# Linear attention and SwiGLU on one core: token tile 2 loaded one weight chunk earlier, its Newton steps on GpSimd, its normalisation behind one more phi(K), a phi(K) and a V cast ahead of its transpose copy

## The chip, the cores and the metric

One core of a Trainium2 chip. The metric is the device time of one execution in microseconds. Each execution is recorded with a state, fast or slow, by its time and the clock granted to TensorE. The profile's span runs from the first to the last instruction; in every profiled run here the device time is about 1.8 us more than the span.

In the profile, PE is TensorE (PEld its weight loads), DVE VectorE, ACT ScalarE, POOL GpSimd and SP SyncE; a q behind a name marks the queue that issues its instructions. PSUM is the memory that the matmuls write to, in banks, and SBUF the one that holds the other tiles on the chip.

## The reference

A linear attention block (32 heads of 32) over a layer-normalised input of 2048 tokens and 1024 features, gated by a SwiGLU block of width 3584:

```python
xn = _layernorm(x)
q, k, v = split_heads(xn @ wqkv)
phi = lambda t: jnp.where(t > 0, t + 1, jnp.exp(t)) + 1e-6
kv = einsum("bhsd,bhse->bhde", phi(k), v);  z = einsum("bhsd->bhd", phi(k))
o  = (phi(q) @ kv) / (phi(q) @ z + 1e-6)
s  = o @ wo
g  = silu((silu(xn @ w_gate) * (xn @ w_up)) @ w_down)
return x + s * g
```

(Shortened here; shapes and the random inputs are left out.)

## The kernel before

Tokens come in 16 tiles of 128, the K/V weights (1024 x 2048) in four chunks of 512 columns: 0 and 1 give K, 2 and 3 give V. For each tile: statistics, 1/sqrt by three Newton steps of four operations each (tiles 0 and 1: by a square root on ScalarE), normalisation, transposition; then for each chunk eight matmuls into a PSUM bank, and an evacuation (phi for K, a cast for V). Below, "product (i, c)" is tile i times chunk c.

The loads, in the order of the sync queue (half of x tile 0 and the whole of x tile 1 go on ScalarE's queue):

```python
load_x(0)
load_x(1)
load_wkv(0, halves=2 if DC % 2 == 0 else 1)
nx = 2
for c in range(1, NCH):
    load_wkv(c)
    if nx < NT and c != 2:
        load_x(nx)
        nx += 1
for i in range(nx, NT):
    load_x(i)
```

Newton, three times, on the engine that is named (GpSimd if none is):

```python
def emit_rstd(gid, eng=None):
    eng = eng or nc.gpsimd
    ...                             # cut: three preparations on nc.vector
    for _ in range(NR_ITERS):       # 3
        eng.tensor_tensor(out=w, in0=y, in1=y, op=ALU.mult)
        eng.tensor_tensor(out=w, in0=w, in1=a, op=ALU.mult)
        eng.tensor_scalar(out=w, in0=w, scalar1=-0.5, scalar2=1.5, op0=ALU.mult, op1=ALU.add)
        eng.tensor_tensor(out=y, in0=y, in1=w, op=ALU.mult)
```

(Slices cut.) Evacuation of K: ScalarE makes `e_t` = exp and `r_t` = relu out of PSUM, which frees the bank; VectorE adds eps to `r_t` and makes `pk_sb` of both, which frees `e_t` and `r_t`. There are two buffers each of `e_t` and `r_t`, and three PSUM banks for products (branches for other tiles are cut):

```python
nc.scalar.activation(out=e_t[:], in_=t_ps, func=ACT.Exp)
nc.scalar.activation(out=r, in_=t_ps, func=ACT.Relu)
nc.vector.tensor_scalar(out=r, in0=r, scalar1=EPS, scalar2=None, op0=ALU.add)
nc.vector.scalar_tensor_tensor(out=dst, in0=e_t[:], scalar=1.0, in1=r, op0=ALU.min, op1=ALU.add)
```

Every engine works through its instructions in the order in which they are emitted. That order at the start of the kernel (what comes before and after is cut):

```python
emit_Bmm(0, 0)          # eight matmuls of tile 0, chunk 0
emit_TR(1)              # transposes on PE, copies out of PSUM
ln_pre(2, nc.vector)    # statistics and Newton of tile 2
emit_Bev(0, 0)          # evacuation
emit_Bmm(1, 0)
emit_N(2)               # normalisation on VectorE
emit_Bmm(0, 1)
emit_Bev(1, 0)
emit_Bev(0, 1)
emit_Bmm(1, 1)
emit_Bmm(0, 2)
emit_TR(2)              # copy out of PSUM on ScalarE
emit_Bev(1, 1)
emit_Bev(0, 2)
emit_Bmm(1, 2)
emit_Bev(1, 2)
ln_pre(3)
emit_Bmm(2, 0)
```

Of the kernel before, what the change touches and what calls it, by code (L numbers as in the profile page):

```python
# [21 lines left out]
def kernel(  # L22
# [11 lines left out]
    nc = tc.nc  # L34
# [7 lines left out]
    NT = S // P  # L42
# [75 lines left out]
    def xn_ap(dcs, tok):  # L118
        b = tok.start // TB
        return xn_blk_tiles[b][:, dcs, tok.start - b * TB:tok.stop - b * TB]  # L120
# [24 lines left out]
    def emit_phi(work, t_ps, dst, W, in_place=False, act=False):  # L145
        e_t = work.tile([P, W], FP32, name="e_t", tag="e_t")
        if act:
            nc.scalar.activation(out=e_t[:], in_=t_ps, func=ACT.Relu, scale=-1.0)
            nc.scalar.activation(out=e_t[:], in_=e_t[:], func=ACT.Exp, scale=-1.0)
            nc.scalar.activation(out=t_ps, in_=t_ps, func=ACT.Relu)  # L150
            phi_late.append(lambda: nc.vector.scalar_tensor_tensor(out=dst, in0=e_t[:], scalar=EPS, in1=t_ps,
                                                                   op0=ALU.add, op1=ALU.add))
            return
        nc.scalar.activation(out=e_t[:], in_=t_ps, func=ACT.Exp)
        if in_place:
            r = t_ps
            nc.vector.tensor_scalar(out=r, in0=t_ps, scalar1=0.0, scalar2=EPS, op0=ALU.max, op1=ALU.add)
        else:
            r_t = work.tile([P, W], FP32, name="r_t", tag="r_t")
            r = r_t[:]  # L160
            nc.scalar.activation(out=r, in_=t_ps, func=ACT.Relu)
            nc.vector.tensor_scalar(out=r, in0=r, scalar1=EPS, scalar2=None, op0=ALU.add)
        nc.vector.scalar_tensor_tensor(out=dst, in0=e_t[:], scalar=1.0, in1=r,
                                       op0=ALU.min, op1=ALU.add)
# [198 lines left out]
    with ExitStack() as p1:  # L363
# [15 lines left out]
        def x_ap(i):  # L379
            return xp_tiles[i // 4][:, i % 4, :]  # L380
# [3 lines left out]
        def load_x(i):  # L384
            if i == 0 and D % 2 == 0:
                h = D // 2
                x_loads[i] = nc.sync.dma_start(out=x_ap(i)[:, 0:h], in_=x2[0:P, 0:h])
                nc.scalar.dma_start(out=x_ap(i)[:, h:D], in_=x2[0:P, h:D])
                return
            if i == 1:  # L390
                x_loads[i] = nc.scalar.dma_start(out=x_ap(i), in_=x2[i * P:(i + 1) * P, :])
                return
            x_loads[i] = nc.sync.dma_start(out=x_ap(i), in_=x2[i * P:(i + 1) * P, :])

        def load_wkv(c, halves=1):
            hs = DC // halves
            return [nc.sync.dma_start(out=wkv_sb[:, h * hs:(h + 1) * hs, c * CW:(c + 1) * CW],
                                      in_=wqkv_v[:, h * hs:(h + 1) * hs, D + c * CW: D + (c + 1) * CW])
                    for h in range(halves)]
# [3 lines left out]
        load_x(0)  # L403
        load_x(1)
        load_wkv(0, halves=2 if DC % 2 == 0 else 1)
        nx = 2
        for c in range(1, NCH):
            load_wkv(c)
            if nx < NT and c != 2:
                load_x(nx)  # L410
                nx += 1
        for i in range(nx, NT):
            load_x(i)
        def load_qo(wt, wv, c):
# [18 lines left out]
        def grp_of(i):  # L433
            return grp_tiles(i)[0]

        def grp_tiles(gid):
            return (gid,) if gid < 6 else (gid - gid % 2, gid - gid % 2 + 1)

        def emit_stats(i):
            gid = grp_of(i)  # L440
            if gid not in grp_state:
                mv = small.tile([P, TPB, AGG], FP32, name="mv", tag="mv")
                rstd = small.tile([P, TPB], FP32, name="rstd", tag="rstd")
                grp_state[gid] = (mv, rstd, grp_tiles(gid))
            mv, rstd, tiles = grp_state[gid]
            k = tiles.index(i)
            stats = small.tile([P, NSC, nc.vector.BN_STATS_DIM], FP32, name="stats", tag="stats")
            xr = x_ap(i).rearrange("p (c f) -> p c f", f=SCH)
            sts = [nc.vector.bn_stats(out=stats[:, c, :], in_=xr[:, c, :]) for c in range(NSC)]
            nc.vector.bn_aggr(out=mv[:, k, :], in_=stats[:])  # L450
            ln_state[i] = (mv, rstd, k)
            return sts
# [31 lines left out]
        def emit_norm(i, dst, cols=None):  # L484
            mv, rstd, k = ln_state[i]
            src = x_ap(i) if cols is None else x_ap(i)[:, cols]
            return nc.vector.tensor_scalar(out=dst, in0=src, scalar1=mv[:, k, 0:1], scalar2=rstd[:, k:k + 1],
                                           op0=ALU.subtract, op1=ALU.mult)
# [3 lines left out]
        def emit_N(i):  # L492
            xn = xnw.tile([P, D], BF16, name="xn", tag="xn")
            xn_tiles[i] = xn
            if i < 2:
                for hh in range(2):
                    cols = slice(hh * (D // 2), (hh + 1) * (D // 2))
                    emit_norm(i, xn[:, cols], cols=cols)
            else:
                emit_norm(i, xn[:])  # L500
            ln_state.pop(i)
            if i >= NPE:
                xn_tiles.pop(i)
                nc.sync.dma_start_transpose(out=xn_ap(slice(0, DC), slice(i * P, (i + 1) * P)), in_=xn[:])

        def emit_TR(i):
            tok = slice(i * P, (i + 1) * P)
            xn = xn_tiles.pop(i)
            nh = 2 if i < 2 else 1
            dch = DC // nh  # L510
            for hh in range(nh):
                tr_ps = psC.tile([P, dch, P], BF16, name="tr_ps", tag="C")
                for dc in range(dch):
                    nc.tensor.transpose(tr_ps[:, dc, :], xn[:, (hh * dch + dc) * P:(hh * dch + dc + 1) * P], ident[:])
                dst = xn_ap(slice(hh * dch, (hh + 1) * dch), tok)
                if i == 1 and hh == 0:
                    nc.vector.tensor_copy(out=dst, in_=tr_ps[:])
                else:
                    nc.scalar.copy(out=dst, in_=tr_ps[:])  # L519
# [5 lines left out]
        def emit_Bmm(i, c):  # L525
            tok = slice(i * P, (i + 1) * P)
            kv_ps = psB.tile([P, CW], FP32, name="kv_ps", tag="B")
            kv_banks[(i, c)] = kv_ps
            for dc in range(DC):
                mm = nc.tensor.matmul(kv_ps[:], lhsT=xn_ap(dc, tok), rhs=wkv_sb[:, dc, c * CW:(c + 1) * CW],  # L530
                                      start=(dc == 0), stop=(dc == DC - 1))
                if dc == 0 and c == 0:
                    marks[("B", i)] = mm

        def emit_Bev(i, c):
            kv_ps = kv_banks.pop((i, c))
            if i not in pkv_tiles:
                pk_sb = work.tile([P, D], BF16, name="pk_sb", tag="pk_sb")
                pkv_tiles[i] = (pk_sb, v_bufs[i % 2])
            pk_sb, v_sb = pkv_tiles[i]  # L540
            if c < NCC:
                emit_phi(phiw, kv_ps[:], pk_sb[:, c * CW:(c + 1) * CW], CW, in_place=i >= 9)
            else:
                vc = c - NCC
                nc.scalar.copy(out=v_sb[:, vc * GPC:(vc + 1) * GPC, 0:P],
                               in_=kv_ps[:].rearrange("p (g c) -> p g c", c=P))
# [10 lines left out]
        def ln_pre(i, eng=None):  # L557
            emit_stats(i)
            if i == grp_tiles(i)[-1]:
                emit_rstd(grp_of(i), eng)  # L560
# [13 lines left out]
        emit_N(1)  # L574
        emit_Bmm(0, 0)
        emit_TR(1)
        ln_pre(2, nc.vector)
        emit_Bev(0, 0)
        emit_Bmm(1, 0)
        emit_N(2)  # L580
        emit_Bmm(0, 1)
        emit_Bev(1, 0)
        emit_Bev(0, 1)
        emit_Bmm(1, 1)
        emit_Bmm(0, 2)
        emit_TR(2)
        emit_Bev(1, 1)
        emit_Bev(0, 2)
        emit_Bmm(1, 2)
        emit_Bev(1, 2)  # L590
        ln_pre(3)
# [845 lines left out]
```

## Time and profile before

| what | value |
|---|---|
| device time, median of the three runs ahead of the prediction | 758.95 us (758.80 to 758.96) |
| the execution that the profile was taken of | 759.85 us, span 758.1 us |
| PE busy | 750.5 us, 99% |
| PE busy before 27 us | 23.75 of 27 us |

The lines that carry the argument stand in the prediction. In a line of a timeline, the first two numbers are start and length in us, then come engine, source line, operation, output<-input, shape and count, and in brackets the idle time of the engine in front of it and what ended it.

### The profile page before, as it was taken

Reading aid. Unit: us, or ns where it says so; the run is one execution under the profiler, and the core shown is the slowest. Engines: PE = TensorE matmul, PEld = TensorE weight load, DVE = VectorE, ACT = ScalarE, POOL = GpSimd, SP = SyncE. Lnnn points to the kernel's source line nnn. Section 1 sums busy time; section 2 is a strip of 40 time slices with the busy share of each in tenths; the row PEclk is TensorE's granted clock in tenths of the full one; section 3 lists DMA queues with packets and bytes.
Section 4 is the critical chain, followed back from the end, with each engine's and each line's share of the span. In section 5 each row is a group of like instructions: output and inputs, shape, how many; then the busy total and the mean of one; then the engine's idle time right before and its main releaser. Section 6 shows DMA issues by size and latency. Waiting matters only on the chain.

```text
span 758.1 us, 10498 instructions
## 1 busy us (share of the span) xinstructions
PE 750.5 (99%) x3731; PEld 348.8 (46%) x3731; DVE 559.8 (74%) x1043; ACT 376.0 (50%) x526; POOL 274.9 (36%) x340
## 2 busy tenths in 40 slices
PE   8999999999999999999999999999999999999997
PEld 3444444454454444444444444444444444444443
DVE  6787787887687778888889775368676777787335
ACT  4678767889966666656658311132323223211122
POOL 0435799998540266868585000100000000200000
PEclk9999999999999999999999999999999999999999
DMA  9767799869688668878799236398644445430824
GB/s 315 256 179 153 198 337 306 311 148 280 198 195 284 229 225 295 296 280 316 265 330 398 106 108 247 125 371 326 230 176 167 167 166 175 178 134 15 278 87 135
DMA packets 105845, 170.30 MB, mean 225 GB/s; under 512 B 34816, under 2 KB 82176, under 8 KB 95168
## 3 DMA queue, kind: packets, MB, share of 16 engines
q1 hardware_dynamic: 100144, 144.99, 59.3%
q0 software_dynamic: 4208, 22.15, 7.5%
q10 hardware_dynamic: 1440, 2.49, 1.0%
q8 instruction: 29, 0.48, 0.3%
q14 instruction: 24, 0.20, 0.1%
HBM read 111.67 MB, written 50.59 MB: 214 GB/s over the span
## 4 chain that ended last, share of the span: by engine, by line
PE 95%; DVE 2%; DMA 1%; ACT 1%; issue 0%; SPq 0%; ACTq 0%; DVEq 0%
PE zw L941 26%; PE kv_ps L530 13%; PE xb L941 13%; PE dzw L1126 12%; PE yb L941 6%; PE q_ps L183 6%; PE dx L1126 6%; PE dy L1126 3%; PE fx L792 3%; PE s_ps L750 3%; DMA xp<-in_A_x_dram 1%; PE kvz L552 1%; PE nd L719 1%; PE df L1126 1%; DVE w_sb L283 0%; PE fx L750 0%
## 5 line engine op out<-in xcount | busy, mean ns | idle before, releaser
L941 PEld LDWEIGHTS <-w_sb 128*128 128x128 f16 (+1 forms) x1568 | 152.2, 98 | 182.7
L941 PE MATMUL xb<-xnT,w_sb 128*128 128x512 bf16 x448 | 115.0, 379 | 0.0
L530 PE MATMUL kv_ps<-wkv_sb,xnT 128*128 128x512 bf16 x512 | 114.0, 379 | 1.0 <-ACT xnT L519 0.5
L941 PE MATMUL zw<-xnT,w_sb 128*128 128x512 bf16 x448 | 105.8, 379 | 0.0
L941 PE MATMUL zw<-S,w_sb 128*128 128x512 f16 x448 | 105.8, 379 | 0.0
L295 POOL TENSOR_TENSOR w_sb<-w_sb 128x512 f16<-128x512 bf16 x42 | 50.2, 1195 | 95.7 <-DVE w_sb L283 51.3
L260 ACT ACTIVATE w_sb<-w_sb 128x2048 bf16<-128x2048 bf16 x42 | 79.9, 1902 | 3.8 <-DMA w_sb<-in_B_w_up_dram 2.8
L1126 PE MATMUL dx<-w_sb,hT 128*128 128x512 bf16 x210 | 79.6, 379 | 0.0
L530 PEld LDWEIGHTS <-xnT 128*128 128x128 bf16 x512 | 48.3, 97 | 56.7 <-ACT xnT L519 0.9
L1126 PEld LDWEIGHTS <-hT 128*128 128x128 bf16 (+1 forms) x462 | 44.7, 98 | 52.3
L183 PE MATMUL q_ps<-xnT,wq_sb 128*128 128x512 bf16 x256 | 58.4, 379 | 0.0
L1126 PE MATMUL dzw<-w_sb,hT 128*128 128x512 f16 x196 | 58.3, 379 | 0.0
L1017 ACT ACTIVATE sg<-cg 128x1024 bf16<-128x1024 f32 x28 | 29.6, 1057 | 57.2 <-DVE cg L1010 57.2
L941 PE MATMUL yb<-S,w_sb 128*128 128x512 f16 x224 | 57.4, 378 | 0.0
L1010 DVE SCALAR_TENSOR_TENSOR cg<-zw,rc_all,s 128x1024 f32<-128x1024 f32 x28 | 35.9, 1284 | 25.9 <-PE zw L941 14.0
L969 DVE SCALAR_TENSOR_TENSOR s<-yb,rc_all,s 128x512 f32<-128x512 f32 x42 | 31.5, 749 | 27.5 <-ACT s L968 27.5
L296 POOL TENSOR_TENSOR w_sb<-w_sb 128x512 f16<-128x512 bf16 x42 | 50.5, 1202 | 3.3
L1066 POOL TENSOR_TENSOR hs<-hT 128x512 f16<-128x512 bf16 x2 | 2.5, 1247 | 132.6 <-ACT sg L1017 132.6
L298 POOL TENSOR_TENSOR w_sb<-w_sb 128x512 f16<-128x512 bf16 x42 | 50.3, 1197 | 0.0
L297 POOL TENSOR_TENSOR w_sb<-w_sb 128x512 f16<-128x512 bf16 x42 | 50.2, 1196 | 0.0
L1100 POOL DMA_DIRECT2D out_dram<-io x16 | 8.7, 542 | 101.9 <-DVE io L1099 101.6
L968 ACT ACTIVATE s<-xb,rcl 128x512 f32<-128x512 f32 x14 | 9.6, 688 | 65.0 <-PE xb L941 65.0
(183 smaller groups left out, 1186.1 us busy)
## 6 DMA issues: line engine op xcount, KB each, us to landing
w_sb<-pk_g SPq DMA_DIRECT2D x27, 1024.0 KB, 5.9
pk_g<-w_sb SPq DMA_DIRECT2D x14, 1024.0 KB, 5.0
w_sb<-wd SPq DMA_DIRECT2D x14, 1024.0 KB, 5.6
w_sb<-pk_u SPq DMA_DIRECT2D x14, 1024.0 KB, 5.0
pk_u<-w_sb POOLq DMA_DIRECT2D x13, 1024.0 KB, 5.4
w_sb<-wd SPq DMA_DIRECT2D x14, 768.0 KB, 5.6
w_sb<-in_B_w_gate_dram SPq DMA_DIRECT2D x14, 512.0 KB, 6.4
w_sb<-in_B_w_down_dram SPq DMA_DIRECT2D x28, 256.0 KB, 4.9
```

The costliest lines, as they stand in the source:

```text
L183: nc.tensor.matmul(q_ps[:], lhsT=wq_sb[:, dc, g * P:(g + 1) * P], rhs=xn_ap(dc, btok), start=(dc == 0), stop=(dc == DC - 1))
L260: nc.scalar.activation(out=junk, in_=raw_view(key, t), func=ACT.Square, accum_out=asum[:])
L295: nc.gpsimd.tensor_tensor(out=T1, in0=b12, in1=b11, op=ALU.subtract)
L296: nc.gpsimd.tensor_tensor(out=T2, in0=b22, in1=T1, op=ALU.subtract)
L297: nc.gpsimd.tensor_tensor(out=T3, in0=b22, in1=b12, op=ALU.subtract)
L298: nc.gpsimd.tensor_tensor(out=T4, in0=b21, in1=T2, op=ALU.subtract)
L530: mm = nc.tensor.matmul(kv_ps[:], lhsT=xn_ap(dc, tok), rhs=wkv_sb[:, dc, c * CW:(c + 1) * CW], start=(dc == 0), stop=(dc == DC - 1))
L941: mm = nc.tensor.matmul(out, lhsT=lhs(k), rhs=rhs(k), start=(first and k == 0), stop=(k == HK - 1), skip_group_check=True)
L969: nc.vector.scalar_tensor_tensor(out=s2[:], in0=y_[:], scalar=rc, in1=s1[:], op0=ALU.mult, op1=ALU.add)
L1010: nc.vector.scalar_tensor_tensor(out=d12, in0=zw[:], scalar=rc, in1=s2[:, None, :].to_broadcast([P, 2, TB]), op0=ALU.mult, op1=ALU.add)
L1017: nc.scalar.activation(out=sg[:, 1:3, :], in_=cf[:], func=ACT.Silu)
L1126: nc.tensor.matmul(out, lhsT=lhs, rhs=rhs, start=first, stop=lastk, skip_group_check=True)
```

## The change

Its intent: let tile 2 arrive earlier, free VectorE of twelve small operations that stand in front of the first phi(K), and let ScalarE free PSUM banks before it copies tile 2's transpose.

```diff
         load_wkv(0, halves=2 if DC % 2 == 0 else 1)
-        nx = 2
+        load_x(2)
+        nx = 3
         for c in range(1, NCH):
             load_wkv(c)
-            if nx < NT and c != 2:
-                load_x(nx)
-                nx += 1
@@
         emit_TR(1)
-        ln_pre(2, nc.vector)
+        ln_pre(2)
         emit_Bev(0, 0)
         emit_Bmm(1, 0)
-        emit_N(2)
         emit_Bmm(0, 1)
         emit_Bev(1, 0)
+        emit_N(2)
         emit_Bev(0, 1)
         emit_Bmm(1, 1)
         emit_Bmm(0, 2)
-        emit_TR(2)
         emit_Bev(1, 1)
         emit_Bev(0, 2)
+        emit_TR(2)
         emit_Bmm(1, 2)
```

The matmuls and transposes of PE keep their order.

## The prediction

> **What bounds the kernel now.** I read the page first (engine shares, then the chain by engine), then busy time by stretch, then the chain in order of time over the start, and last the timelines of PE, DVE and GpSimd (POOL) around the edited code.
>
> From the page, parts 1 and 4:
>
> ```profile
> PE 750.5 (99%) x3731; PEld 348.8 (46%) x3731; DVE 559.8 (74%) x1043; ACT 376.0 (50%) x526; POOL 274.9 (36%) x340
> PE 95%; DVE 2%; DMA 1%; ACT 1%; issue 0%; SPq 0%; ACTq 0%; DVEq 0%
> ```
>
> The reader is to see that PE bounds the kernel: 95% of the chain that ended last. So a change of this kind, which removes no matmul, can only win idle time of PE. Busy time by stretch says where that is:
>
> ```profile
> 0.00:27.00 27.00, 23.75 (x123) 10.86 (x124) 16.62 (x58) 12.31 (x21) 2.90 (x20) 1.00 1.00 333
> 27.00:150.00 123.00, 123.00 (x694) 60.11 (x692) 100.32 (x218) 94.23 (x154) 91.39 (x140) 1.00 0.83 241
> ```
>
> (The columns after the length are busy time of PE, PEld, DVE, ACT, POOL; then clock, DMA share and GB/s.) From 27 to 150 us PE is never idle; before 27 us it lacks 3.25 us. The edit touches only this first stretch. What it wins there, the dense stretch behind it hands on unchanged, since everything later is tied to matmuls and not to the clock on the wall.
>
> The chain in order of time, start us and length us:
>
> ```profile
> 2.75 9.32 DMA xp<-in_A_x_dram
> ...
> 12.10 1.30 DVE stats L449 x2
> ...
> 16.52 0.35 DVE r_t L162
> 16.89 0.70 DVE pk_sb L163
> ...
> 17.69 0.60 ACT e_t L154
> ...
> 20.26 0.50 ACT r_t L161
> ...
> 20.80 5.34 PE kv_ps L530 x24
> ```
>
> The chain is not on PE before 20.80. It is: token tile 2 lands at 12.08; its statistics and Newton steps hold DVE, in order, until 16.5; only then DVE makes the first phi(K) (pk_sb), which frees the buffer that ACT's next exponential waits for, and ACT in turn frees the PSUM banks. PE's timeline shows what that costs:
>
> ```profile
> 10.20 7.08 PE L530 MATMUL kv_ps<-wkv_sb,xnT 128*128 128x512 bf16 x32 [0.30 <-DVE xnT L517]
> 18.09 0.62 PE L514 MATMUL tr_ps<-ident,xn 128*128 128x128 bf16 x8 [0.81 <-DVE xn L487]
> 18.83 7.31 PE L530 MATMUL kv_ps<-wkv_sb,xnT 128*128 128x512 bf16 x32
> ```
>
> A matmul takes 0.38 us but follows its forerunner after (7.08-0.38)/31 = 0.216 us; a transpose after (0.62-0.22)/7 = 0.057. So 32 matmuls from 10.20 let PE go on at 17.11; the transposes of tile 2 start at 18.09 (0.98 lost, waiting for the normalised tile). They would let PE go on at 18.55; it starts at 18.83 (0.28 lost, bank still read by ACT). Eight matmuls later, at 20.56, tile 2's first product could start, and the chain has it at 20.80 (0.24 lost, bank again). **Lost: 1.50 us.** That is the most that these parts of the change can win.
>
> **What the Trainium skill says.** "Perfetto Trace Analysis", section "Identifying the Most-Contended Engine": matmul busy share is a poor measure of headroom because matmuls are pipelined. The trace agrees: PE's busy row charges only 0.81 us to the transposes' wait, the starts show 0.98, and the two bank waits are in no row. Hence I reckon in start times.
>
> "DMA: Bandwidth & Descriptors", section "Queues, rings and completion order": on each DMA engine descriptors are consumed in ring order. So an earlier issue on the same queue means an earlier landing, paid by whatever it overtook. The trace agrees: tile 2, issued right behind chunk 1 of the K/V weights, landed 0.7 us after it (below).
>
> "SBUF — State Buffer", section "Who interferes with whom": a DVE instruction with two SBUF inputs, or in a 2-port mode, and a GpSimd one that reads SBUF exclude each other for a whole instruction. The trace agrees; DVE and POOL timelines:
>
> ```profile
> 30.25 0.69 DVE L163 SCALAR_TENSOR_TENSOR pk_sb<-e_t,r_t 128x512 bf16<-128x512 f32 x1
> 30.26 0.72 POOL L479 TENSOR_TENSOR lnw<-lnw,lna 128x1 f32<-128x1 f32 x1
> ```
>
> Usually the same POOL step takes 0.19. So Newton steps on POOL beside phi(K) on DVE will be stretched.
>
> **The change part by part.**
>
> Part 1, the load order. Two weight chunks, each alone in its stretch of the DMA view (size, us to landing): chunk 1, issued at 2.21, and chunk 2, issued at 4.31.
>
> ```profile
> wkv_sb<-in_A_wqkv_dram SPq DMA_DIRECT2D x1, 1024.0 KB, 9.2
> wkv_sb<-in_A_wqkv_dram SPq DMA_DIRECT2D x1, 1024.0 KB, 10.8
> ```
>
> Chunk 1 lands at 11.4, tile 2 at 12.08 (2.75+9.32), chunk 2 at 15.1. The second half of chunk 0 (issued 1.66, 6.7 to landing) is there at 8.4. Swapped, tile 2 lands at about 8.4+0.7 = 9.1 and chunk 1 at 12.08; bytes in front of chunk 2 are the same, so all later loads stay. Chunk 1 is first needed by the ninth of the 32 matmuls, at 10.20+8x0.216 = 11.93. Now it starts at about 12.12: **0.19 us of new wait**.
>
> Part 2, statistics. DVE's last work before them is the copy of tile 1's transpose, which ends at 10.14. They start at 10.16 instead of 12.10, 1.94 us earlier.
>
> Part 3, Newton. On DVE the twelve steps run from 14.23 to 16.52, so leaving takes 2.3 us out of DVE's queue. On POOL, tile 3's undisturbed run gives the price:
>
> ```profile
> 24.03 0.19 POOL L478 TENSOR_TENSOR lnw<-rstd 128x1 f32<-128x1 f32 x1 [22.65 <-DVE rstd L474]
> ...
> 27.03 0.19 POOL L482 TENSOR_TENSOR rstd<-rstd,lnw 128x1 f32<-128x1 f32 x1
> ```
>
> That is 0.273 us a step against 0.193 on DVE. The last DVE preparation starts at 14.04-1.94 = 12.10, the first POOL step 0.24 later (as 23.79 to 24.03) at 12.34, the last 3.00 later, and the normalisation 0.22 after that (27.03 to 27.25): 15.56 undisturbed. But DVE now does four phi(K) operations in that time: ACT's relus end at 12.92 and 13.91, so DVE works from 12.95 to about 15.2. Tile 4's POOL run, beside the same four operations, took 4.16 us between first and last step (29.88 to 34.04) instead of 3.00. That gives 16.72; laying the steps against the four operations one by one gives 16.87. I take 16.8. The normalisation lasts 0.54, so tile 2 is ready at 17.35.
>
> Part 4, the order of emission. Normalising tile 2 behind tile 1's first phi(K) keeps DVE from idling in front of phi(K) while POOL works. Moving tile 2's transpose copy on ACT behind the phi of (tile 1, chunk 1) and the V cast of (tile 0, chunk 2) gives PSUM banks back first. PE's own order is unchanged. Check of the path: the first phi(K) is done at 14.1 (before: 17.6), ACT's next exponential starts there and its bank is free at 15.3; the next pair ends at about 16.9; the V cast at about 18.1 (0.41 behind the last matmul, as 24.04 to 24.45, plus 0.6); the transpose copy takes 1.01 more, to about 19.1.
>
> Sum for PE: matmuls 9 to 32 run from 12.12 to 17.30. Transposes start at 17.40, 0.05 after the tile is ready (0.10 lost). The next eight matmuls start at 17.86 (bank free since 15.3). Tile 2's first product starts at 19.59; its copy ended at 19.1, its bank at 16.9. Before it was 20.80: **1.2 us won** of the 1.50, with 0.19 lost to the weights and 0.10 to POOL. 758.95-1.2 = 757.75; I say **757.7 us**.
>
> Behind that I looked for something that does not move. Chunk 3 lands at 18.1 and is needed at 21.3; tile 3 is in by 19; its normalisation gets earlier. Tile 4 comes by DMA transpose: it landed at 38.0, needed at 40.0, and its input also gets earlier. Nothing there takes the gain back.
>
> **The rivals.** (a) Weights take the place of the tile: chunk 1 comes later than 12.12, say 12.6 to 13, because the longer issue stalls on the sync queue (tile 2's issue took 1.5 us, chunk 3's 3.9) hit it. For: PE has only 0.5 us of slack there now. Against: issue is far ahead of landing. It would leave 0.5 to 0.9 us: 758.0 to 758.4. (b) POOL becomes the bound: the steps end at 17.5 or later, through the lock or a slow start after long idling. For: the 0.72 us steps. Against: tile 3's first step, after 22.6 us of idling, took 0.19. It would leave 0.3 to 0.6 us: 758.4 to 758.6. (c) POOL is hardly disturbed and PE waits only for the weights: 1.3 us, 757.6. (d) The gain is given back later, because a later stage waits for something timed from the start: 758.9. Against: the dense stretch to 150 us.
>
> **Range and chances.** (a) and (b) set the upper end, 758.6; the lower, 757.1, allows the full 1.5 us and a few tenths of shuffling later. The three runs before lie within 0.16 us. Two per cent is 15 us, over four times all the idle time in the first stretch, so within 2% is near certain: faster 0.01, same 0.98, slower 0.01.
>
> **What would show it.** In the changed profile: tile 2's statistics at about 10.2; the ninth matmul of the row at 10.20 starting near 12.1, with a wait for the weights' DMA; POOL steps from about 12.3 to 16.6, some of 0.3 to 0.7 us; transposes at about 17.4; tile 2's first product at about 19.6, with PE dense from there to 149 us. I am wrong if the ninth matmul starts after 12.5, the transposes after 17.8, if the copy on ACT makes tile 2's first product wait, or if PE shows new idle time later.

## The result, and the profile after

The changed kernel took 758.28 us in the median of six runs (757.82 to 758.50), the kernel before 758.89 (758.75 to 758.96) beside it. The ratio is 0.9991, with a 95% interval of 0.9978 to 1.0004: the same within 2%, and inside the predicted range. The interval takes in 1, though no run of one kernel overlaps with one of the other. A ratio is the mean time of one kernel's fast runs over that of the other's of the same rounds, so not quite the ratio of the medians. The medians differ by 0.6 us, half of the 1.2 that I had worked out, yet the two spans differ by 1.4 us (758.1 and 756.7). That contradiction is what the experiments are about.

The chain of the changed kernel, in order of time:

```profile
10.24 3.19 PE kv_ps L528 x14
13.49 3.83 PE kv_ps L528 x17
17.32 0.57 PE tr_ps L512 x8
17.89 5.40 PE kv_ps L528 x25
```

From 10.24 on the chain is on PE. The token load, the statistics, the phi and ScalarE's exponentials, which made it up before, are gone from it. PE, VectorE and GpSimd in the timelines:

```profile
10.24 7.08 PE L528 MATMUL kv_ps<-wkv_sb,xnT 128*128 128x512 bf16 x31 [0.30 <-DVE xnT L515]
17.27 0.62 PE L512 MATMUL tr_ps<-ident,xn 128*128 128x128 bf16 x8
17.72 7.07 PE L528 MATMUL kv_ps<-wkv_sb,xnT 128*128 128x512 bf16 x31
...
10.10 1.28 DVE L447 BATCH_NORM_STATS2 stats<-xp 128x6 f32<-128x512 bf16 x2
16.66 0.55 DVE L485 TENSOR_SCALAR xn<-xp,mv,rstd 128x1024 bf16<-128x1024 bf16 x1 [1.45 <-POOL rstd L480]
...
12.27 0.19 POOL L476 TENSOR_TENSOR lnw<-rstd 128x1 f32<-128x1 f32 x1 [10.89 <-DVE rstd L472]
13.55 0.65 POOL L476 TENSOR_TENSOR lnw<-rstd 128x1 f32<-128x1 f32 x1
16.44 0.19 POOL L480 TENSOR_TENSOR rstd<-rstd,lnw 128x1 f32<-128x1 f32 x1
```

The transposes start 0.05 us after tile 2 is normalised (16.66+0.55 = 17.21), and PE could have gone on at 10.24+32x0.216 = 17.15: 0.12 us lost, to GpSimd. The next eight matmuls follow without a wait, and product (2, 0) starts at 19.45, eight pitches of 0.216 behind 17.72. (A count of 31 where 32 were issued is a missing record: this trace has 3662 matmuls to 3731 weight loads. So its PE busy time of 746.6 us doesn't show idleness, and I compare starts.)

Landing of the loads after, each line alone in its stretch of the DMA view (KB each, us from issue to landing): chunk 0's second half, issued at 1.67; tile 2, issued at 2.21; chunk 1, issued at 2.75.

```profile
wkv_sb<-in_A_wqkv_dram SPq DMA_DIRECT2D x1, 512.0 KB, 5.8
xp<-in_A_x_dram SPq DMA_DIRECT2D x1, 256.0 KB, 6.0
wkv_sb<-in_A_wqkv_dram SPq DMA_DIRECT2D x1, 1024.0 KB, 8.4
```

So they land at 7.5, 8.2 and 11.2. The first of these is not touched by the change, and yet it was at 8.4 in the first trace of the kernel before. The two executions did not begin alike.

### The profile page after: what moved, and what is told of

It reads as the page before. It is cut to its first block, busy times and chain, and to the rows that moved or that the text cites. A ratio compares the mean times of both kernels' runs of the same rounds, so it can differ in the third digit from the quotient of the medians.

```text
span 756.7 us, 10426 instructions
## 1 busy us (share of the span) xinstructions
PE 746.6 (99%) x3662; PEld 349.0 (46%) x3731; DVE 558.5 (74%) x1031; ACT 376.3 (50%) x526; POOL 278.4 (37%) x352
## 4 chain that ended last, share of the span: by engine, by line
PE 97%; DVE 1%; ACT 1%; issue 1%; ACTq 0%; DVEq 0%
PE zw L939 26%; PE kv_ps L528 15%; PE xb L939 13%; PE dzw L1124 12%; PE yb L939 6%; PE q_ps L183 6%; PE dx L1124 6%; PE dy L1124 3%; PE fx L790 3%; PE s_ps L748 2%; PE kvz L550 1%; PE nd L717 1%; PE df L1124 1%; PE warm_ps L564 1%; DVE w_sb L283 0%
## 5 line engine op out<-in xcount | busy, mean ns | idle before, releaser
L939 PE MATMUL xb<-xnT,w_sb 128*128 128x512 bf16 x420 | 113.3, 379 | 1.5
L1124 PE MATMUL dx<-w_sb,hT 128*128 128x512 bf16 x202 | 76.6, 379 | 0.3
L1124 PE MATMUL dzw<-w_sb,hT 128*128 128x512 f16 (+1 forms) x190 | 57.0, 379 | 0.0
```

Source lines behind the costliest of these rows:

```text
L939: mm = nc.tensor.matmul(out, lhsT=lhs(k), rhs=rhs(k), start=(first and k == 0), stop=(k == HK - 1), skip_group_check=True)
L1124: nc.tensor.matmul(out, lhsT=lhs, rhs=rhs, start=first, stop=lastk, skip_group_check=True)
```

## The experiments

**Theory A**: the profiled execution of the kernel before had late loads. In that kernel time follows tile 2's landing one for one, so a typical execution lost much less than 1.5 us, and the change wins only that. **Theory B** (the rival): the profile was typical, and the changed kernel gives 0.7 us back somewhere behind 27 us. The other runs take the change apart.

The kernels of e1 to e4 ran on one chip, those of e5 to e8 on a second, those of e9 to e12 on a third, each group with nine runs of the kernel before and five of each kernel.

### e1: the kernel before, unchanged

> The kernel before, unchanged, for a second trace. Its first trace comes from an execution of 759.85 us, 0.9 us over its timed runs. Theory A (that one execution had late weights: the second half of K/V chunk 0 landed at 8.4 there and at 7.5 in the trace after): now chunk 0's second half lands near 7.5, token tile 2 near 11.2 instead of 12.08, the transposes of tile 2 start near 17.5 instead of 18.09, tile 2's first product near 20.2 instead of 20.80, span about 757.1. Theory B (the first trace was typical and the changed kernel gives 0.7 us back somewhere behind 27 us in its timed runs): tile 2 lands at 12.0 to 12.1 again, first product near 20.8, span about 758. Time against the kernel before: 1.000 in both.

Measured: 759.07 us (758.72 to 760.07) beside 759.24 (758.89 to 760.18), ratio 0.9999. The profiled execution was one of 758.77 us. Its chain and its PE timeline:

```profile
2.76 8.27 DMA xp<-in_A_x_dram
...
15.82 0.70 DVE pk_sb L163
...
19.74 2.32 PE kv_ps L530 x10
```

```profile
10.12 7.08 PE L530 MATMUL kv_ps<-wkv_sb,xnT 128*128 128x512 bf16 x32 [0.30 <-DVE xnT L517]
17.04 0.61 PE L514 MATMUL tr_ps<-ident,xn 128*128 128x128 bf16 x8
17.76 3.43 PE L530 MATMUL kv_ps<-wkv_sb,xnT 128*128 128x512 bf16 x14
```

Tile 2 landed at 11.03, not 12.08, and the first phi(K) began at 15.82, not 16.89. PE was free at 10.12+6.91 = 17.03, so the transposes waited for nothing. Left were the two waits for banks: 17.76 instead of 17.04+0.45 = 17.49, and (2, 0) at 19.74 instead of 17.76+1.73 = 19.49. Together 0.5 us are lost where the first trace had 1.5. Same program, 1.1 us of span apart. Theory A is borne out, as far as a second trace can; I had put the transposes 0.5 us and (2, 0) 0.5 us too late.

### e2: the whole change again

> The whole change once more. Theory A: ratio about 0.9992 (0.6 us), tile 2's first product at 19.5 to 19.7 and PE as dense behind it as in its first trace. Theory B: the same ratio, but the trace shows PE idle time behind 27 us that the kernel before doesn't have. Spread among its runs some 0.7 us, as in the first six.

Measured: 758.13 us (758.09 to 758.29), ratio 0.9984 (0.9971 to 0.9996). Chunk 0's second half came late this time (8.1), tile 2 at 8.8 and chunk 1 at 11.8, and yet (2, 0) started at 19.32 and the span was 756.5. The change doesn't mind a late start of this size. On this chip the kernel before was slower and more scattered than on the others, so the gain is 1.2 us in the means (759.37 and 758.16), twice what I expected, and the spread of its runs, 0.20 us, is far under the 0.7 expected.

### e3: only the load order

```diff
-        nx = 2
+        load_x(2)
+        nx = 3
         for c in range(1, NCH):
             load_wkv(c)
-            if nx < NT and c != 2:
-                load_x(nx)
-                nx += 1
```

> Only the load order of the change; Newton stays on VectorE ahead of the first phi(K), transpose copy ahead of the phi of tile 1. If an early tile 2 is what pays: statistics at 10.1, Newton done on VectorE near 14.4, first phi(K) done near 15.5, no wait at the transposes, but the transpose copy in front of tile 1's exponential keeps a PSUM bank until about 20.0, so tile 2's first product waits some 0.5 us and starts near 20.0: 0.2 us faster than before, 758.7. If the load order alone does it all: as the whole change, 758.3.

Measured: 758.54 us (758.41 to 758.69), ratio 0.9989 (0.9977 to 1.0002). ScalarE and PE:

```profile
17.60 1.01 ACT L517 COPY xnT<-tr_ps 128x1024 bf16<-128x1024 bf16 x1 [1.05 <-PE tr_ps L512]
...
19.66 1.67 PE L528 MATMUL kv_ps<-wkv_sb,xnT 128*128 128x512 bf16 x7 [0.36 <-ACT r_t L161]
```

The transposes wait for nothing any more (16.96). But ScalarE, in order, stands idle for 1.05 us until PE has transposed, copies, and only then makes tile 1's second exponential, and (2, 0) waits for that bank: 19.66 instead of 17.40+1.73 = 19.13, so 0.5 us. The mechanism is as expected. In its trace as much is lost as in e1's (0.53 us), in one bank wait instead of two: beside an execution with early loads the new load order alone wins nothing. The gain, 0.8 us in the means on this chip, is more than the 0.2 that I wrote. By theory A that is because most executions of the kernel before had later loads there than the traced one, but no trace of them shows it. Against the whole change it is short by 0.4 us in the means, as the bank wait says. Its five runs lie within 0.28 us and those of e2 within 0.20, while the kernel before beside them ranges over 1.3 us.

### e4: only the moves between engines, loads as before

The edit is the change without its first hunk.

> Only the moves between engines of the change, the loads as before. If tile 2's landing is the root: it lands near 11.2, Newton runs on GpSimd from 13.4 to 17.6 beside phi(K), tile 2 is ready near 18.2, its transposes start near 18.3 (1.2 us lost) and its first product at 20.4 to 20.5: 0.2 to 0.3 us slower than before, 759.1 to 759.2. If the load order doesn't matter: as the whole change, 758.3.

Measured: 759.31 us (759.27 to 761.09), ratio 1.0004 (0.9992 to 1.0017). Tile 2 landed at 11.2, and PE says:

```profile
18.32 0.62 PE L514 MATMUL tr_ps<-ident,xn 128*128 128x128 bf16 x8 [1.61 <-DVE xn L487]
```

Without the early load, the slower steps on GpSimd are added behind the landing: statistics at 11.24, last Newton step at 17.49, tile 2 ready at 18.26. The bank waits are gone, but (2, 0) starts at 20.50, 0.8 us later than in e1. In time this kernel isn't told from the one before. One of its five runs took 761.09 us; the other four lie within 0.24.

### e5: the change without the move of the transpose copy

```diff
         emit_Bmm(0, 2)
+        emit_TR(2)
         emit_Bev(1, 1)
         emit_Bev(0, 2)
-        emit_TR(2)
```

> The whole change, but tile 2's transpose copy on ScalarE stays ahead of tile 1's second exponential, as before. If the copy's place is one of the parts that pay: no wait at the transposes, but the copy waits for them until about 17.8, tile 1's exponential and relu follow until about 19.8, and tile 2's first product waits some 0.4 us for that PSUM bank: 0.4 us slower than the whole change, like the load order alone (758.5). If early tile 2 and GpSimd are all that counts: as the whole change, 758.1.

Measured: 758.86 us (758.53 to 759.19), ratio 0.9998 (0.9986 to 1.0011).

```profile
19.50 5.34 PE L528 MATMUL kv_ps<-wkv_sb,xnT 128*128 128x512 bf16 x24 [0.36 <-ACT r_t L161]
```

The wait of e3 is back: (2, 0) at 19.50 instead of 17.25+1.73 = 18.98, 0.5 us. In time nothing is left of the gain (758.86 in both medians). The copy's place is the second part that pays.

### e6 and e12: the change with Newton left on VectorE

```diff
-        ln_pre(2)
+        ln_pre(2, nc.vector)
```

> The whole change, but Newton stays on VectorE. If the move to GpSimd pays (it takes 2.3 us out of VectorE's queue): slower than the whole change by 0.2 to 0.4 us. If with tile 2 landed early that time was hidden anyway: VectorE ends Newton near 14.3, both phi(K) pairs near 16.4, tile 2 is ready near 16.9 (about as on GpSimd), the copy ends near 19.0, no wait: equal to the whole change within 0.1 us. I expect the second.

> Newton on VectorE, otherwise the whole change, on the same chip as the change. If the move to GpSimd is worth nothing in time: equal to the change within 0.1 us. If it pays or costs: apart by 0.2 us or more.

Measured: e6 758.09 us (757.79 to 758.47), ratio 0.9989; e12 758.00 us (757.78 to 758.14), ratio 0.9987 (0.9974 to 0.9999), beside e11 with the whole change on the same chip at 758.34 (757.90 to 758.75), 0.9991. PE in e6:

```profile
16.76 0.61 PE L512 MATMUL tr_ps<-ident,xn 128*128 128x128 bf16 x8
17.20 7.07 PE L528 MATMUL kv_ps<-wkv_sb,xnT 128*128 128x512 bf16 x32
```

From (1, 0) at 9.84 to (2, 0) at 18.93 there are 9.09 us, which is 32x0.216+0.45+8x0.216: PE loses nothing at all. The whole change loses 0.12 us at its transposes in the first trace and about as much in e2 and e11. So the move to GpSimd wins nothing here; the trace has it costing 0.1 us. The timed medians on one chip lie 0.34 us apart, more than I expected, but the runs overlap; I take no more from them than the sign.

### e7: load order and copy alone

Like e6, but `emit_N(2)` stays where it was, between the phi(K) of tile 0 and of tile 1.

> The two parts alone that seem to matter: the load order and the place of the transpose copy; Newton on VectorE and the normalisation at its old place between the phi(K) of tiles 0 and 1. If the place of the normalisation doesn't matter: as the whole change within 0.1 us. If it does: the second phi(K) ends near 16.9 instead of 16.4, the copy near 19.4, and tile 2's first product waits some 0.2 us: 758.3 against 758.1. I expect the second, with little confidence.

Measured: 758.46 us (758.37 to 758.77), ratio 0.9995 (0.9982 to 1.0007).

```profile
19.45 5.35 PE L528 MATMUL kv_ps<-wkv_sb,xnT 128*128 128x512 bf16 x24 [0.24 <-ACT xnT L517]
```

The normalisation pushes tile 1's phi(K) 0.5 us back, ScalarE's next exponential waits for its buffer, the copy ends at 19.39, and (2, 0) waits: 19.45 instead of 17.32+1.73 = 19.05, 0.4 us, twice what I had written. So the place of the normalisation counts too, in concert with the copy.

### e8: tile 2 one weight chunk later

```diff
-            if nx < NT and c != 2:
+            if nx < NT and c != 1:
```

> The kernel before with token tile 2 one weight chunk later (behind K/V chunk 2 instead of chunk 1), which makes it land some 3.0 us later, near 14.1. Theory A (in the kernel before, time follows tile 2's landing one for one, so the spread of its runs is spread of landing): 2.8 to 3.1 us slower, ratio about 1.0039, the transposes of tile 2 near 20.1, chunk 2 near 13.4. If something else sets the start and the landing is hidden: 0 to 1 us slower.

Measured: 763.23 us (761.67 to 763.42) beside 758.86, ratio 1.0052 (1.0039 to 1.0066). The chain and PE:

```profile
4.04 10.62 DMA xp<-in_A_x_dram
14.68 1.30 DVE stats L449 x2
...
23.37 2.75 PE kv_ps L530 x12
```

```profile
20.66 0.62 PE L514 MATMUL tr_ps<-ident,xn 128*128 128x128 bf16 x8 [3.33 <-DVE xn L487]
```

Tile 2 landed at 14.65 (4.04+10.62), 0.5 us later than expected. Three traces of the old order of work now stand in a row: landing 11.03, 12.08, 14.65 us; span 756.97, 758.07, 760.63 us. That is 1.10 us of span for 1.05 us of landing, and 2.56 for 2.57. One for one, as theory A says. In time the loss is 3.9 us in the means, more than the 2.8 to 3.1 expected; the profiled run of this kernel, at 762.45, is one of its faster ones. By theory A the landings of the others were later still, but no trace of them shows it.

### e9, e10 and e11: an attempt to beat both kernels

Tile 1's transposes in halves, the first half between the sixth and the seventh matmul of (0, 0), so that (1, 0) starts sooner; e9 with Newton on VectorE as in e6, e10 on the change as it is:

```diff
-        emit_Bmm(0, 0)
-        emit_TR(1)
+        emit_Bmm(0, 0, range(6))
+        emit_TR(1, (0,))
+        emit_Bmm(0, 0, range(6, DC))
+        emit_TR(1, (1,))
```

> An attempt at a version that beats the change: Newton on VectorE as in e6, and the first half of tile 1's transposes moved in between the sixth and seventh matmul of tile 0's first product, so that tile 1's first product starts near 9.85 instead of 10.0 to 10.2. Tile 2 is ready near 16.9 either way, so PE should wait 0.1 at its transposes: 0.1 to 0.3 us faster than the whole change. If chunk 1 of the weights now arrives too late (needed near 11.6, landing 11.2 to 11.8): no gain.

> The same split on the whole change with Newton on GpSimd. If GpSimd's stretched steps are close to being the bound (tile 2 is ready near 17.1 in the change, PE free at 17.1 to 17.3): PE frees at 16.8 and waits some 0.2 to 0.3 us at the transposes, so equal to the change within 0.1 us and slower than the split with VectorE. If they have slack: 0.2 to 0.3 us faster than the change.

> The whole change once more, to stand beside the others on one chip: 0.6 to 1.1 us faster than before (758.1 to 758.3), spread of its runs smaller than that of the kernel before.

Measured, on one chip: e9 757.88 us (757.61 to 758.15), ratio 0.9986 (0.9973 to 0.9998); e10 757.87 (757.68 to 758.17), 0.9985 (0.9971 to 0.9999); e11 758.34 (757.90 to 758.75); the kernel before 758.92. Both are about 0.4 us faster than the change in the means, with overlapping runs, so this is likely and not proved. From (0, 0) to (1, 0) it is 2.24 us in e9 (7.47 to 9.71), 2.57 in e10, whose first half waited for tile 1's normalisation, and 2.64 in e11 with the change. So the earlier start accounts for 0.07 us in e10's trace, the wait at the transposes of tile 2 for 0.15 (table below), and the rest of the 0.4 isn't traced. The first branch of my expectation for e10, a new wait for GpSimd, did not come:

```profile
16.19 0.55 DVE L485 TENSOR_SCALAR xn<-xp,mv,rstd 128x1024 bf16<-128x1024 bf16 x1 [0.91 <-POOL rstd L480]
...
16.80 0.62 PE L514 MATMUL tr_ps<-ident,xn 128*128 128x128 bf16 x8
```

I had kept GpSimd's end at 17.1 and moved only PE. But the copy of tile 1's first half comes earlier too (9.40 instead of 9.76), so statistics and Newton start earlier, and tile 2 is ready at 16.74, just ahead of PE. GpSimd is near the bound, not the bound.

### All traces in one table

Starts in us, read from the timelines: product (1, 0), transposes of tile 2, product (2, 0). "Lost" is the third minus the first minus 9.09, the time of the work between them. The last column is the span minus the start of (2, 0).

| trace | (1, 0) | transposes | (2, 0) | lost | span | behind (2, 0) |
|---|---|---|---|---|---|---|
| before, first | 10.20 | 18.09 | 20.80 | 1.51 | 758.07 | 737.27 |
| e1 before, again | 10.12 | 17.04 | 19.74 | 0.53 | 756.97 | 737.23 |
| the change, first | 10.24 | 17.27 | 19.45 | 0.12 | 756.72 | 737.27 |
| e2 change, again | 10.11 | 17.14 | 19.32 | 0.12 | 756.51 | 737.19 |
| e3 load order only | 10.04 | 16.96 | 19.66 | 0.53 | 756.88 | 737.22 |
| e4 engine moves only | 9.63 | 18.32 | 20.50 | 1.78 | 757.72 | 737.22 |
| e5 no copy move | 9.77 | 16.80 | 19.50 | 0.64 | 756.74 | 737.24 |
| e6 Newton on VectorE | 9.84 | 16.76 | 18.93 | 0.00 | 756.18 | 737.25 |
| e7 load order and copy | 9.96 | 16.87 | 19.45 | 0.40 | 756.98 | 737.53 |
| e8 tile 2 later | 10.24 | 20.66 | 23.37 | 4.04 | 760.63 | 737.26 |
| e9 split, Newton on VectorE | 9.71 | 16.63 | 18.81 | 0.01 | 756.08 | 737.27 |
| e10 split on the change | 9.88 | 16.80 | 18.98 | 0.01 | 756.25 | 737.27 |
| e11 change, third | 9.81 | 16.87 | 19.06 | 0.16 | 756.33 | 737.27 |
| e12 Newton on VectorE, again | 9.99 | 16.91 | 19.08 | 0.00 | 756.36 | 737.28 |

The last column is the answer to theory B: behind (2, 0) every kernel takes 737.2 to 737.3 us, whatever happened in front, so the changed kernel gives nothing back. (e7 is 0.3 us off in its one trace. That trace has a wait that those of e3 and e6 don't have: at 169.71 a product of Q found PE idle for 0.37 us behind VectorE's `pqT`. Why it came is open.) The start of (1, 0) varies by 0.6 us between executions, and that of (0, 0) by 0.7 (6.91 to 7.60). What sets them I didn't examine; the change doesn't touch it, but it is part of every time.

## Why the prediction was right or wrong

The time was inside the range, and nearly all steps hold, but that the number fell inside was in part luck. The upper part of the range was there for rivals (a) and (b). Neither came, and yet 758.28 is where (a) would have put it (758.0 to 758.4); the reason is the last point below.

- **What bounds the kernel, and that later stages hand the gain on unchanged**: right, and exact to 0.1 us in the table, e7 aside.
- **Load order**: the swap was right in size (tile 2 lands 0.7 us behind chunk 0's second half, chunk 1 3.0 us later), but both came 0.9 us sooner than I wrote, because the base execution was late. So the new wait of 0.19 us for chunk 1 didn't show: it landed at 11.2 and was needed at 11.97. In e2 it landed at 11.80 and was needed at 11.84, so the slack does get used up. That an earlier issue means an earlier landing was the prediction's own step: the cited section speaks of the order in which descriptors are consumed. These traces bear it out, in the changed kernel with 7.5, 8.2, 11.2, 14.2 and 17.2 us in the order of issue. Rival (a) did not occur in these traces.
- **Statistics at 10.16**: 10.10. **GpSimd from 12.34 to 16.5**: 12.27 to 16.44. **Stretched steps**: 0.65 us where 0.19 is usual. **Normalisation at 16.8**: 16.66. **0.10 us lost at the transposes to GpSimd**: 0.12; luck in part, as both sides came 0.15 us sooner than I wrote, PE because it didn't wait for chunk 1 (free at 17.15, not 17.30) and the tile because it started 0.06 us sooner and GpSimd was stretched a little less (ready at 17.21, not 17.35). Rival (b) is there in this size only.
- **Order on ScalarE**: right; e3 and e5 each show the 0.5 us wait for the bank that it takes away. That the place of the normalisation matters was only argued in the prediction, as keeping VectorE from idling; e7 shows it with VectorE doing Newton as well, where it is the copy that comes late.
- **Newton on GpSimd**: the prediction booked "2.3 us out of DVE's queue" as the thing that part wins. e6 and e12 show that with tile 2 early this time was hidden already.
- **The term that was mis-sized is the base: "Lost: 1.50 us".** I read it from the profile of an execution of 759.85 us and took the gain off the median of 758.95. From the slow execution the sum is right: its span less 1.2 is 756.9, and 756.7 and 756.5 were measured. The second traced execution of the kernel before, e1's, loses 0.53 us there, and the change 0.12 to 0.16 in three traces, so about 0.4 us of gain is traced. Measured was 0.6 us in the medians of the first rounds and of e11's, 1.1 on the chip of e2. Executions whose tile 2 landed later than e1's would make up the rest by theory A; none of the timed ones shows it, so the rest stays open. The difference between profiled run and median stood in the times before the prediction, and I passed over it.

So the change does two things: it takes away a loss of some 0.5 us at the banks that all three traces of the old order of work have (the first, e1 and e8), at the price of the 0.1 us that GpSimd costs; and it takes tile 2's landing off the path, which cost nothing in e1 and 1.0 us in the first trace. Chunk 1 of the weights stands next in line, with 0.04 us to spare in e2.

## What to carry to other kernels

Compare the time of the profiled execution with the median before taking a gain out of its trace: a wait on the first loads may be that execution's own. Where PE is dense behind some point, one number, the start of the work at that point, tells what an edit at the beginning is worth, and the span behind it shows whether anything is given back. A move to another engine isn't worth something because it relieves a busy engine: try the edit without it (here it cost 0.1 us in the trace).

## What the Trainium skill lacked or had wrong

- "DMA: Bandwidth & Descriptors", section "Queues, rings and completion order", gives the order of descriptors but nothing on how much landings differ between executions of one program. The same half chunk of weights, issued as the same fifth transfer at 1.66 to 1.67 us, landed at 8.4 us in one trace of the kernel before and at 7.3 in the other (7.3 to 8.4 in all fourteen traces), and in these two the next four loads on that queue shifted with it, by 1.0 to 1.1 us.
- "GPSIMD Engine Reference", section "Performance versus the Vector engine", compares the engines for 2048 elements (1.96 times). For the 128x1 steps here the pitch was 0.273 us on GpSimd and 0.193 on VectorE, 1.4 times, as long as VectorE was quiet.
- "SBUF — State Buffer", section "Who interferes with whom", says that whichever comes second at the shared ports is fully blocked, and the trace of the changed kernel agrees: beside a VectorE operation of 0.69 us (13.46 to 14.15) a step that takes 0.19 us elsewhere took 0.65 and ended at 14.20. It has no figure for a chain of short steps: twelve of them beside four VectorE operations, two of 0.69 us and two of about 0.42, took 4.2 us from first to last start instead of 3.0.
